# A gated linear attention and two-stage MoE kernel: half of each attention result computed on the other head's partitions and moved back by DMA

## The chip, the cores and the metric

The kernel runs on one core of a Trainium2 chip. A core has a matmul engine (TensorE, PE in the rows; its weight loads are PEld), three elementwise engines (VectorE = DVE, ScalarE = ACT, GpSimd = POOL), a queue engine that here issues nearly all transfers (SyncE = SP), and 16 DMA engines that move the data. The metric is device microseconds of one execution.

## The reference, cut to what matters

```python
for t in range(S):                                   # B=4, H=8, S=768, D=48
    state = alpha[:, :, t, :, None] * state + einsum('bhd,bhe->bhde', k[:, :, t], v[:, :, t])
    y[:, :, t] = einsum('bhd,bhde->bhe', q[:, :, t], state)
x = y.transpose(0, 2, 1, 3).reshape(3072, 384)
x = ((x @ w1) * (x @ w2)) @ w3 @ w_out               # widths 384 -> 1024 -> 1024 -> 384
p = probs / (probs.sum(-1) + 1e-9)
out = sum_e p[:, e] * (relu(x @ ew1[e]) @ ew2[e])    # 4 experts, 384 -> 1024 -> 384
```

## The kernel before

Every large product runs in three passes: a float32 operand is split into a high and a low part (hi by a copy on ACT, lo by a subtraction on DVE or POOL), and `mm3` (L86, L87, L88) adds hi*hi, lo*hi and hi*lo into one PSUM bank.

**Attention.** The sequence is cut into 24 chunks of 128 tokens (4 batches times 6). One chunk holds 8 heads as 4 pairs `p`; of a pair, head g=0 lies on partitions 0 to 63 and head g=1 on 64 to 127. A chunk is treated in two halves `t` of 64 tokens. For a chunk `i`: two scans on DVE give the decay products W (L574) and P (L582); k and q are scaled by them (`kW` L588, `qP` L592); k is transposed on PE (`kps`, L607) and copied (`kT`, L612); `u` (L632, tile `su`) makes the state updates and `scores` (L621, also `su`) makes q*k; DVE adds the updates into the states Zh and Z (L657, L664) and masks the scores into the tile `s` (L683). The output `y` (tile `yps`, one PSUM bank for each half t) gets two parts: `inter` (L673), old state times q, and `sv` (L691), masked scores times v. In `inter` head g reads its own partitions and writes its own partitions of `y`, and the loop has t outermost. ACT then copies y as the hi part (L707) and DVE subtracts for the lo part (L710), both straight into `xt`, the input of the next products. After a tile of three chunks, `pack` (L718) moves the padding rows of xt by six small DMAs, two for each of the three k-slices.

From chunk index 6 on (`GROUPED`) the PE work of a chunk comes as one group: `inter` of chunk i-1, `u` and `scores` of chunk i, `sv` of chunk i-1. There are 18 such chunks.

**First products.** A tile `j` of 384 tokens (8 tiles) gives 16 units of 9 matmuls (`abps`): x@w1 and x@w2 for 8 slices f. ACT copies a (L772), DVE multiplies (L776) into `g_sb`, which is stored to DRAM (`spilled`, L779). w1 and w2 arrive as wide words that are converted in 8 pieces on DVE and ACT (`c_m` L141, L142, L147; `w1h`, `w1l`, `w2h`, `w2l`), as later w_out and w3 (`wps`). Then `xps` makes x of the second stage, which is stored in sums as `kept`.

**Experts.** From about 440 us on the loop over 32 blocks (4 experts, 4 token tiles, 2 parts of the width) runs: `hps` are the first products by a scheme with fewer multiplications (the sums are on DVE, L1294), `ops` the second ones. The expert's weights are loaded, summed and split in `load_a`; the split goes in the pieces that `W_STEPS` lists (L1024, L1026). `checks` test that the inputs lie in the range that this fast path supports; `held_out` (L1160, L1161) reduces the outcome to one flag by a matmul into a bank of the `hps` pool, and at the very end all engines load that flag and branch.

**Order of the work.** Up to the expert loop a planner (`Plan`) sets each engine's instruction order: each operation has a cost and a due time made of the constants in the table at `TILE_DUE`; at each step it takes the ready operation with the earliest due time. The order is fixed when the program is built. The transfers of SP are one queue in that order, so an instruction that waits there holds all behind it.

## Time and profile before

| | |
|---|---|
| median of 3 runs | 1196.91 us (1194.83 to 1200.28) |
| the profiled execution's own time | 1197.35 us |
| its span, first to last instruction | 1195.5 us |
| PE busy | 1167.1 us, 98% |
| DVE, ACT, POOL busy | 69%, 52%, 37% |
| mean granted TensorE clock | 0.993 of full |

The span is what the profiler saw between the first and the last instruction; the execution's own time is 1.85 us longer. Busy shares are averages over stages, and a busy PE is a modelled figure (matmuls overlap), so stages and single chunks have to be read one by one.

### The profile page before, as it was taken

What the parts mean: (1) busy time and instruction counts of PE and PEld (TensorE: products, weight loads), DVE (VectorE), ACT (ScalarE), POOL (GpSimd) and SP (SyncE); (2) the same over time, 40 slices, a digit from 0 to 9 for tenths busy, and PEclk for the clock granted to TensorE, in tenths of its full rate; (3) what the DMA queues carried; (4) which work ended last, traced back from release to release, by engine and by line L of the source; (5) the groups of instructions that cost most, each with busy time, mean ns of one, the idle gap of its engine ahead of it and who ended that gap; (6) DMA issues with size and microseconds to landing.
All of it is one profiled execution on the core that took longest, in us unless ns stands there. A gap on an engine that the chain in (4) does not pass through costs nothing.

```text
span 1195.5 us, 24960 instructions
## 1 busy us (share of the span) xinstructions
PE 1167.1 (98%) x9186; PEld 1149.3 (96%) x9186; DVE 829.2 (69%) x1513; ACT 627.4 (52%) x1238; POOL 445.1 (37%) x517
## 2 busy tenths in 40 slices
PE   5899999999999999999999999999999999999997
PEld 4799999999999999999999999999999999999997
DVE  8898788966665856667677656667666587576563
ACT  4565555554544445454666655666565545444432
POOL 2133321010000006776744434744433655433332
PEclk9899999999999999999999999999999999999999
DMA  8756675555775696478576595695784863753821
GB/s 318 223 171 188 211 216 200 173 166 192 272 284 177 243 337 226 168 304 292 208 288 225 199 330 203 244 347 178 275 303 156 307 244 127 290 176 142 291 81 43
DMA packets 131171, 269.54 MB, mean 225 GB/s; under 512 B 17376, under 2 KB 64992, under 8 KB 131040
## 3 DMA queue, kind: packets, MB, share of 16 engines
q1 hardware_dynamic: 130176, 266.67, 63.8%
q8 instruction: 75, 1.23, 0.4%
q10 hardware_dynamic: 864, 1.18, 0.3%
q14 instruction: 56, 0.46, 0.1%
HBM read 207.24 MB, written 58.20 MB: 222 GB/s over the span
## 4 chain that ended last, share of the span: by engine, by line
PE 95%; DVE 3%; DMA 1%; issue 0%; POOL 0%; SPq 0%; ACT 0%; DVEq 0%; POOLq 0%
PE ops L87 11%; PE ops L86 11%; PE ops L88 11%; PE hps L86 9%; PE hps L87 9%; PE hps L88 9%; PE abps L86 6%; PE abps L87 6%; PE abps L88 6%; PE xps L86 3%; PE xps L88 3%; PE xps L87 3%; PE yps L673 2%; PE yps L691 1%; PE wps L86 1%; PE wps L88 1%
## 5 line engine op out<-in xcount | busy, mean ns | idle before, releaser
L1294 DVE TENSOR_TENSOR raw_x<-hps,raw_x 128x384 f32<-128x384 f32 x416 | 226.4, 554 | 212.3 <-PE hps L88 197.2
L1277 POOL TENSOR_TENSOR ht<-raw_x,ht 128x384 fp32r<-128x384 f32 x227 | 238.1, 1051 | 274.5 <-ACT raw_x L1276 222.2
L1275 ACT ACTIVATE ht<-raw_x 128x384 fp32r<-128x384 f32 x227 | 118.6, 523 | 228.3 <-DVE raw_x L1294 215.9
L87 PE MATMUL ops<-wb,ht 128*128 128x384 f32 x681 | 231.5, 340 | 0.0
L86 PE MATMUL ops<-wb,ht 128*128 128x384 f32 x681 | 230.8, 339 | 0.0
L88 PE MATMUL ops<-wb,ht 128*128 128x384 f32 x681 | 230.6, 339 | 0.0
L86 PE MATMUL hps<-xo,wa 128*128 128x384 f32 x640 | 217.8, 340 | 2.5 <-DVE raw_x L1294 1.2
L87 PE MATMUL hps<-xo,wa 128*128 128x384 f32 x640 | 215.5, 337 | 0.0
L88 PE MATMUL hps<-xo,wa 128*128 128x384 f32 x640 | 215.1, 336 | 0.0
L1294 DVE TENSOR_TENSOR raw_x<-raw_x,hps 128x384 f32<-128x384 f32 x256 | 136.5, 549 | 25.5 <-PE hps L88 25.1
L1276 ACT ACTIVATE raw_x<-raw_x 128x384 f32<-128x384 f32 x256 | 134.7, 526 | 8.1
L86 PEld LDWEIGHTS hps<-xo,wa 128*128 128x128 f32 x640 | 120.2, 188 | 8.4 <-DVE raw_x L1294 6.0
L86 PEld LDWEIGHTS ops<-wb,ht 128*128 128x128 f32 x681 | 128.0, 188 | 0.0
L88 PEld LDWEIGHTS ops<-wb,ht 128*128 128x128 f32 x681 | 127.9, 188 | 0.0
L87 PEld LDWEIGHTS ops<-wb,ht 128*128 128x128 f32 x681 | 127.5, 187 | 0.0
L87 PEld LDWEIGHTS hps<-xo,wa 128*128 128x128 f32 x640 | 120.2, 188 | 0.0
L88 PEld LDWEIGHTS hps<-xo,wa 128*128 128x128 f32 x640 | 120.1, 188 | 0.0
L1294 DVE TENSOR_TENSOR raw_x<-raw_x 128x384 f32<-128x384 f32 x128 | 88.6, 692 | 4.4
L698 POOL MEMSET Z<- 128x1 f32 x18 | 1.8, 98 | 191.7 <-PE yps L673 191.7
L1277 POOL TENSOR_TENSOR ho<-raw_x,ho 128x384 fp32r<-128x384 f32 x29 | 30.7, 1060 | 105.0 <-DMA xo<-kept 71.4
L86 PE MATMUL abps<-xt,w2h 128*128 128x384 f32 x192 | 66.0, 344 | 0.0
L86 PE MATMUL abps<-xt,w1h 128*128 128x384 f32 x192 | 65.9, 343 | 0.0
(136 smaller groups left out, 2224.2 us busy)
## 6 DMA issues: line engine op xcount, KB each, us to landing
xo<-kept SPq DMA_DIRECT2D x272, 384.0 KB, 6.4
kept<-ac SPq DMA_DIRECT2D x45, 384.0 KB, 2.9
partial<-ac SPq DMA_DIRECT2D x72, 192.0 KB, 1.9
ac<-partial SPq DMA_DIRECT2D x72, 192.0 KB, 6.4
spilled<-g_sb SPq DMA_DIRECT2D x64, 192.0 KB, 2.3
gg<-spilled SPq DMA_DIRECT2D x64, 192.0 KB, 3.3
c_raw<-in_w3T_dram SPq DMA_DIRECT2D x16, 512.0 KB, 4.1
raw_x<-in_w3T_dram SPq DMA_DIRECT2D x8, 1024.0 KB, 7.0
```

Source lines behind the costliest of these rows:

```text
L86: nc.tensor.matmul(out=ps, lhsT=lh, rhs=rh, start=first, stop=False)
L87: nc.tensor.matmul(out=ps, lhsT=ll, rhs=rh, start=False, stop=False)
L88: nc.tensor.matmul(out=ps, lhsT=lh, rhs=rl, start=False, stop=last)
L673: PE.matmul(out=r["y"][rows, p, t], lhsT=Z[rows, p], rhs=r["q"][rows, p, half], start=p == 0, stop=False)
L691: PE.matmul(out=r["y"][rows, p, t], lhsT=v[half, p, g], rhs=r["s"][half, g, p], start=first and t == 0 and p == 0, stop=p == NP - 1)
L698: G.memset(r["Zh"][:, NP - 1, 63:], 0.0)
L1275: A.activation(out=hh[:, 0], in_=s, func=ACTF.Relu)
L1276: A.activation(out=s, in_=s, func=ACTF.Relu)
L1277: G.tensor_tensor(out=hh[:, 1], in0=s, in1=f32(hh[:, 0]), op=ALU.subtract)
L1294: V.tensor_tensor(out=tmp[:, s], in0=ins[0], in1=ins[1], op=SIGN[op])
```

## The change

1. **Other head's partitions.** In grouped chunks, the second half's results (t=1) of head g are written on the partitions of the other head: `rows2[g ^ (t & grouped)]` in `inter` and `sv`. `inter` now goes over the heads outermost and the halves inside.
2. **Moving back.** The first half's hi and lo are made as before, 256 columns wide. The second half's go into the memory of the chunk's score tile `s`, which has been read by then (`turned`), and two DMAs on SP (`swap`) put them into xt. `masked` of the chunk after next, `pack` and the products wait for them.
3. **Weight splits** in 12 pieces instead of 8 (`W_STEPS`), with the loop's slots for them extended to 12.
4. **`held_out`** is called after the last matmul block instead of when the checks end.
5. **Last stores**: of the last six, three go on ACT's queue and three on SP's.
6. **A new table** of due times, which reorders all that the planner orders.

```diff
-W_STEPS = ((0, 0, 6), (0, 6, 12), (1, 0, 6), (0, 12, 16), (1, 6, 12), (0, 16, 20), (1, 12, 16), (1, 16, 20))
+W_STEPS = ((0, 0, 3), (0, 3, 6), (1, 0, 3), (0, 6, 9), (1, 3, 6), (0, 9, 12), (1, 6, 9), (0, 12, 16), (1, 9, 12),
+           (0, 16, 20), (1, 12, 16), (1, 16, 20))
...
-CHUNK_DUE = 72150.5
-ATT_DUE = -6421.33
+CHUNK_DUE = 81059.4
+ATT_DUE = 133025
...
-                n["u"] = n["scores"] = add("PE", (0.36 + 0.18 + 0.18 * (not last) + 0.47) + (1.39 if i > GROUPED else 0), due + U_DUE,
+                n["u"] = n["scores"] = add("PE", (0.36 + 0.18 + 0.18 * (not last) + 0.47) + (0.94 if i > GROUPED else 0), due + U_DUE,
...
-                for t, half in halves[first:]:
-                    Z = r["Zh"] if t else tiles[i - B]["Z"]
-                    for p, g, rows in heads:
-                        PE.matmul(out=r["y"][rows, p, t], lhsT=Z[rows, p], rhs=r["q"][rows, p, half],
+                for p, g, rows in heads:
+                    for t, half in halves[first:]:
+                        Z = r["Zh"] if t else tiles[i - B]["Z"]
+                        PE.matmul(out=r["y"][rows2[g ^ (t & grouped)], p, t], lhsT=Z[rows, p], rhs=r["q"][rows, p, half],
...
-            n["m"] = add("DVE", dve(512) + 0.07, due + M_DUE, masked, n["scores"], n.get("inter"), old(2, "sv"), port=False)
+            n["m"] = add("DVE", dve(512) + 0.07, due + M_DUE, masked, n["scores"], n.get("inter"), old(2, "sv", "swap"),
+                         port=False)
...
-                            PE.matmul(out=r["y"][rows, p, t], lhsT=v[half, p, g], rhs=r["s"][half, g, p],
+                            PE.matmul(out=r["y"][rows2[g ^ (t & grouped)], p, t], lhsT=v[half, p, g],
+                                      rhs=r["s"][half, g, p],
...
+            def parts():
+                x = tiles["x", j][:, :, :, o * C:(o + 1) * C].rearrange("p s n (t e) -> p s n t e", t=2)
+                if not grouped:
+                    return [(x, r["y"])]
+                turned = r["s"].rearrange("p g n e -> p (g n e)").bitcast(F32R).rearrange("p (s n e) -> p s n e", s=2, n=NP)
+                return [(x[:, :, :, 0], r["y"][:, :, 0]), (turned, r["y"][:, :, 1])]
...
-                A.activation(out=x[:, 0], in_=r["y"], func=ACTF.Copy)
+                for x, y in parts():
+                    A.activation(out=x[:, 0], in_=y, func=ACTF.Copy)
...
-                V.tensor_tensor(out=r["x"][:, 1], in0=r["y"], in1=f32(r["x"][:, 0]), op=ALU.subtract)
+                for x, y in parts():
+                    V.tensor_tensor(out=x[:, 1], in0=y, in1=f32(x[:, 0]), op=ALU.subtract)
+
+            def swap():
+                (x, _), (turned, _) = parts()
+                x = tiles["x", j][:, :, :, o * C + HC:(o + 1) * C]
+                for g in range(2):
+                    nc.sync.dma_start(out=f32(x[rows2[g]]), in_=f32(turned[rows2[1 - g]]))
...
+                if grouped:
+                    n["swap"] = add("SP", 2 * 0.65, due + HI_DUE, swap, n["lo"], kib=256)
...
-            x_in = [at[i][k] for i in range(j * CPT, (j + 1) * CPT) for k in ("pack", "lo") if k in at[i]]
+            x_in = [at[i][k] for i in range(j * CPT, (j + 1) * CPT) for k in ("pack", "lo", "swap") if k in at[i]]
...
             V.tensor_reduce(out=over, in_=excess, axis=mybir.AxisListType.X, op=ALU.add)
-            yield
-            held_out()
...
-                (nc.scalar if t == NT2 - 1 else nc.sync).dma_start(out=out[r * 128:(r + 1) * 128], in_=ac)
+                (nc.scalar if t == NT2 - 1 and m % 2 == 0 else nc.sync).dma_start(out=out[r * 128:(r + 1) * 128], in_=ac)
...
             second(*block)
+        held_out()
```

Of the new table only two lines are shown; its effect is seen in the orders. On PE, where the third tile (j=2, chunks 6 to 8) begins, the order of before has 63 `abps` matmuls between the groups of chunks 10 and 11; `Z_106` and `Z_110` are the two states that `inter` of chunk 10 reads (below, its end; further `abps` rows are left out):

```order
L691 MATMUL yps<-s,rv 64x64 x16
L86 MATMUL abps<-xt,w1h 128x384
...
L607 MATMUL kps<-ident,rk 128x128 x4
L673 MATMUL yps<-rq,Z_106 64x64 x8
L673 MATMUL yps<-rq,Z_110 64x64 x8
L632 MATMUL su<-rv,kT 64x48 x16
L621 MATMUL su<-rq,rk 64x64 x16
L691 MATMUL yps<-s,rv 64x64 x16
```

The order of the change has the same place, with the two groups back to back and two transposes between them:

```order
L633 MATMUL su<-rv,kT 64x48 x16
L622 MATMUL su<-rq,rk 64x64 x16
L693 MATMUL yps<-s,rv 64x64 x16
L608 MATMUL kps<-ident,rk 128x128 x8
L674 MATMUL yps<-rq,Z_106 64x64
L674 MATMUL yps<-rq,Z_110 64x64
...
L633 MATMUL su<-rv,kT 64x48 x16
L622 MATMUL su<-rq,rk 64x64 x16
L693 MATMUL yps<-s,rv 64x64 x16
L87 MATMUL abps<-xt,w1h 128x384
```

The group of chunk 11 has moved ahead of the third tile's first products (ten units, 90 matmuls, now follow it), and `inter` alternates between the two states, which is the alternation between the halves.

On SP's queue at the same place, before (the names in brackets are the semaphores that the issue waits for):

```order
L553 DMA rk<-in_kT_dram 128x512 [waits DMAHW0_49]
L718 DMA xt<-xt 16x2x384 [waits DMAHW1_49,DVE_49]
L718 DMA xt<-xt 16x2x384 [waits DMAHW2_49]
L718 DMA xt<-xt 16x2x384 [waits DMAHW3_49]
L718 DMA xt<-xt 16x2x384 [waits DMAHW4_49]
L718 DMA xt<-xt 16x2x384 [waits DMAHW5_49]
L718 DMA xt<-xt 16x2x384 [waits DMAHW6_49]
```

and with the change:

```order
L727 DMA xt<-s 64x8x64 [waits DMAHW5_49,DVE_49,Activation_49]
L727 DMA xt<-s 64x8x64 [waits DMAHW6_49]
L799 DMA spilled<-g_sb 128x384 [waits DMAHW7_49,DVE_49]
L1134 DMA p_sb<-in_probs_dram 128x24x4 [waits DMAHW0_49]
L735 DMA xt<-xt 16x2x384 [waits DMAHW5_49,DMAHW1_49]
L735 DMA xt<-xt 16x2x384 [waits DMAHW6_49,DMAHW2_49]
L735 DMA xt<-xt 16x2x384 [waits DMAHW3_49]
L735 DMA xt<-xt 16x2x384 [waits DMAHW4_49]
L735 DMA xt<-xt 16x2x384 x2
L799 DMA spilled<-g_sb 128x384 [waits DMAHW7_49,DVE_49]
L727 DMA xt<-s 64x8x64 [waits DVE_49,DMAHW0_49,PE_49,Activation_49]
L727 DMA xt<-s 64x8x64 [waits DMAHW1_49]
```

The six DMAs of `pack` waited for DVE's lo part; now they wait for the landing of the two swaps ahead of them, and the swaps wait for DVE.

On DVE, ahead of the first products of the kernel (the end of chunk 3's lo part, `xt`, and what stands beside it), before:

```order
L683 TENSOR_TENSOR s<-su,mask 128x512
L141 TENSOR_SCALAR c_m<-c_raw 128x768
L142 SCALAR_TENSOR_TENSOR c_m<-c_raw,c_m 128x768
L657 TENSOR_TENSOR Z_110<-su,Z_105 128x4x48
L664 TENSOR_TENSOR Z_109<-su,Z_110 128x4x48
L710 TENSOR_TENSOR xt<-yps,xt 128x4x128
L582 SCALAR_TENSOR_TENSOR P<-ra,edge 128x520
```

and with the change:

```order
L684 TENSOR_TENSOR s<-su,mask 128x512
L583 SCALAR_TENSOR_TENSOR P<-ra,edge 128x520
L658 TENSOR_TENSOR Z_110<-su,Z_105 128x4x48
L665 TENSOR_TENSOR Z_109<-su,Z_110 128x4x48
L721 TENSOR_TENSOR xt<-yps,xt 128x4x128
L96 TENSOR_TENSOR w1l<-c_m,w1h 128x3x256
```

Chunk 5's scan P has moved ahead of chunk 3's lo part, and the low part of the first weights (`w1l`), which stood well ahead of it, now follows it; the second conversion (`c_m`) is further up.

## Rows read from the trace of the kernel before

**Rows 1.** The page, part 1: busy us, share of the span, instructions.
```profile
PE 1167.1 (98%) x9186; PEld 1149.3 (96%) x9186; DVE 829.2 (69%) x1513; ACT 627.4 (52%) x1238; POOL 445.1 (37%) x517
```

**Rows 2.** Windows: stretch, its length, busy PE, PEld, DVE, ACT, POOL, clock, DMA.
```profile
100.00:200.00 100.00, 100.00 (x1604) 96.99 (x1603) 81.56 (x142) 55.46 (x130) 27.16 (x36) 1.00 0.69 209
...
600.00:800.00 200.00, 200.00 (x1133) 198.33 (x1132) 135.97 (x253) 118.62 (x214) 97.59 (x115) 1.00 0.71 257
```

**Rows 3.** Waits of PE: us in total, times, longest.
```profile
PE yps L673 <- DVE xt L710: 6.8, 4, 2.8
...
PE hps L86 <- DVE held L1161: 0.5, 1, 0.5
```

**Rows 4.** The chain that ended last, one attention group: start, us, what.
```profile
84.06 1.01 PE yps L673 x29
...
85.53 0.48 PE su L621 x28
86.07 0.47 PE yps L691 x30
86.54 0.38 PE abps L86
...
91.42 0.44 PE kps L607 x4
...
103.26 0.47 PE yps L691 x30
...
111.54 0.38 PE abps L86
```

**Rows 5.** Groups by line and form: busy us, mean ns, idle before.
```profile
L710 DVE TENSOR_TENSOR xt<-yps,xt 128x512 fp32r<-128x512 f32 x24 | 16.4, 684 | 4.8 <-ACT xt L707 4.5
L707 ACT ACTIVATE xt<-yps 128x512 fp32r<-128x512 f32 x24 | 14.3, 596 | 23.9 <-PE yps L691 22.0 <-PE abps L87 0.9 <-DMA ra<-in_aT_dram 0.9
...
L657 DVE TENSOR_TENSOR Z<-su,Z 128x192 f32<-128x192 f32 x20 | 7.0, 351 | 9.9 <-PE su L621 9.9
...
L655 ACT ACTIVATE Z<-su 128x192 f32<-128x192 f32 x4 | 1.3, 319 | 1.2 <-PE su L621 1.1
```

**Rows 6.** Timeline of PE: two starts, nine matmuls apart.
```profile
53.47 0.33 PE L86 MATMUL abps<-xt,w1h 128*128 128x384 f32 x1
...
55.03 0.34 PE L86 MATMUL abps<-xt,w2h 128*128 128x384 f32 x1
```

**Rows 7.** SP's timeline at the third tile; landing times of pack; issues.
```profile
105.40 4.16 SPq L718 DMA_DIRECT2D xt<-xt  x6
...
DMA to landing us min/median/max: 2.1/2.5/4.9
...
rv<-in_vP_dram SPq DMA_DIRECT2D x24, 256.0 KB, 3.9
...
p_sb<-in_probs_dram SPq DMA_DIRECT2D x1, 48.0 KB, 4.0
```

**Rows 8.** Timeline of DVE and of PE before the first products.
```profile
25.77 1.31 DVE L95 TENSOR_TENSOR w1l<-c_m,w1h 128x768 fp32r<-128x768 f32 x1
...
38.11 0.68 DVE L710 TENSOR_TENSOR xt<-yps,xt 128x512 fp32r<-128x512 f32 x1
38.71 1.23 DVE L582 TENSOR_TENSOR_SCAN P<-ra,edge 128x520 f32<-128x520 f32 x1
...
38.94 1.97 PE L673 MATMUL yps<-rq,Z 64*64 64x64 f32 x32 [0.52 <-DVE xt L710]
40.84 0.69 PE L86 MATMUL abps<-xt,w1h 128*128 128x384 f32 x1
```

**Rows 9.** Groups by line and form: the split of an expert's weights on DVE.
```profile
L1024 DVE TENSOR_TENSOR wa<-araw,wa 128x768 fp32r<-128x768 f32 x10 | 9.4, 951 | 0.0
```

**Rows 10.** Timeline of the end, DVE and ACT's queue.
```profile
1189.00 0.61 DVE L1246 SCALAR_TENSOR_TENSOR ac<-ops,p_sb,ac 128x384 f32<-128x384 f32 x1
1189.02 1.91 ACTq L1250 DMA_DIRECT2D out_dram<-ac  x4
```

More of the change, by code (lines that the diff above doesn't have):

```diff
@@ L334 @@
 MM = 0.174
[L335 to L381 removed]
+TILE_DUE = 145492
+CHUNK_DUE = 81059.4
+ATT_DUE = 133025
+START_DUE = -9.24766e+07
+START_STEP = 2.61366e+06
+NEXT_DUE = -8.97403e+06
+NEXT_STEP = 12775.5
+LOAD_DUE = 146577
+UNIT_DUE = 24975.8
+ZS_DUE = -994399
+CHECK_DUE = 890180
+KT_DUE = -87820.2
+U_DUE = -43145.3
+Z_DUE = -968641
+M_DUE = -11914.3
+KW_DUE = -4.37131e+06
+QP_DUE = 1.74468e+06
+HI_DUE = 5223.09
+SC_DUE = 178459
+IN_DUE = -335253
+CONV_DUE = 106678
+CONV_STEP = 9690.71
+RAW_DUE = -7.01133e+06
+WO_DUE = 1.2661e+08
+W3_DUE = 742416
+W3_STEP = 939.36
+WL_DUE = 674141
+WL_STEP = 1.47992e+07
+XS_DUE = -26816.4
+XS_STEP = 193058
+XT_DUE = 204116
+XT_STEP = 674192
+XU_DUE = 834547
+XU_STEP = 79170.5
+X0_DUE = 207605
+X1_DUE = 283836
+X2_DUE = -94266.6
+X3_DUE = -5397.31
+X4_DUE = 1.18092e+06
+X5_DUE = 10660.2
+X6_DUE = 912612
+X7_DUE = 852795
+XA_DUE = 207213
+XL_DUE = 1.26613e+08
+XL_STEP = 2.34819e+07
+G_LEAD = 1.27588e+06
+FIRST_DUE = 28655.7
 EARLY = 3
@@ L721, in rest @@
             def rest():
-                n["hi"] = add("ACT", act(512), due + HI_DUE, hi, n["sv"], ab_done.get(j - 2))
-                n["lo"] = add("DVE", dve(512), due + HI_DUE, lo, n["hi"], port=False)
+                n["hi"] = add("ACT", (1 + grouped) * act(512 // (1 + grouped)), due + HI_DUE, hi, n["sv"], ab_done.get(j - 2))
+                n["lo"] = add("DVE", (1 + grouped) * dve(512 // (1 + grouped)), due + HI_DUE, lo, n["hi"], port=False)
+                if grouped:
+                    n["swap"] = add("SP", 2 * 0.65, due + HI_DUE, swap, n["lo"], kib=256)
                 if o == CPT - 1:
-                    n["pack"] = add("SP", 6 * 0.65, due + HI_DUE, pack, [at[k]["lo"] for k in range(i - CPT + 1, i + 1)],
+                    n["pack"] = add("SP", 6 * 0.65, due + HI_DUE, pack,
+                                    [at[k].get("swap", at[k]["lo"]) for k in range(i - CPT + 1, i + 1)],
                                     kib=288)
@@ L735, in final @@
                     sv()
-                n["inter"] = n["sv"] = add("PE", 2.1, due + HI_DUE, final, n["m"], n["Zh"], n["qP"], old(1, "lo"))
+                n["inter"] = n["sv"] = add("PE", 1.65, due + HI_DUE, final, n["m"], n["Zh"], n["qP"], old(1, "lo"))
                 rest()
@@ L1213, in gated_attention_moe_kernel @@
                     job(load_a(e, k), (i0 - 4 + k, 18), *((i0 - 3 + k, g) for g in range(19)),
-                        *((i0 - 1 + k, g) for g in (1, 2, 3, 4, 5, 6, 7, 9)))
+                        *((i0 - 1 + k, g) for g in range(1, 13)))
                 job(load_b(e, 0), (i0 - 1, 0))
```

46 lines of the change are left out of this document (removed).

## The prediction

> **What bounds the kernel now.** I read the page's first part, then the windows, then PE's waits, then the chain. The first part says that PE is busy for 1167.1 us, 98% of the span, and that no other engine comes near it [rows 1]. The windows say where: from 100 to 200 us, where attention runs between the first products, and from 600 to 800 us, in the expert loop, PE has no idle time at all, while DVE has 18 us and 64 us of it in the same stretches [rows 2]. What is left for others is the start. The longest waits of `inter` on DVE's lo part sum to 6.8 us in 4 waits [rows 3], and the one of them that I show ends at 38.9 us [rows 8]. So the rule for this kernel is simple: in the first 40 us DVE counts, at the very end the last stores count, and in between a microsecond taken off PE's instructions is a microsecond of the kernel, as long as the new order doesn't make PE wait.
>
> **Part 1, `inter` on four quadrants.** One group, in the chain: `inter` 1.01 us, `scores` 0.48, `sv` 0.47, and with `u` from 84.06 to 86.54, that is 2.48 us [rows 4]. `inter` and `sv` are alike in number and shape (16 matmuls of 64x64, two passes each), yet `inter` takes twice as long. What differs is where they lie: `inter` alternates between two quadrants of the array (head 0 to its own partitions, head 1 to its own), and both neighbours write the same bank; `scores` and `sv` go round all four quadrants. The change sends `inter` round all four and alternates the banks. `sv` keeps four. I take the 0.48 of `scores`, whose loop (pair, head, half) is the nearest to the new one: 0.53 us less for a chunk, 18 chunks, **-9.5 us**. Bounds: 0.47 as `sv` would give -9.7; if the quadrants aren't the reason, 0.
>
> The Trainium skill, "TensorEngine Tiling (Array Packing)", has two sentences for this. Under "Key Properties" different tiles run in parallel, and by that alone the two diagonal quadrants of before should have overlapped already, which 1.01 against 0.47 [rows 4] denies. Under "Restrictions and Gotchas" different row tiles can't access one PSUM bank at the same time, and this fits the trace: before, neighbours of different row tiles share a bank. After it each bank is still written from both row tiles, two matmuls apart, so by that rule only neighbours overlap: half of 1.01 is 0.505, a sum of 9.1 us in place of 9.5.
>
> **Part 2, hi and lo in two halves.** DVE takes 351 ns for 192 columns and 684 for 512 [rows 5], about 418 for 256, so twice 418 in place of 684: 0.15 us more. ACT takes 319 and 596 [rows 5], about 374 for 256: also 0.15 more. Over 18 chunks that is 2.7 us on each engine, in a stage where DVE has 18 idle us in a hundred and ACT 44 [rows 2]: nothing on the path, except inside the chain of part 3.
>
> **Part 3, swap and pack at a tile's start.** Before, the way from a tile's last `sv` to its first product was: `sv` ends at 103.26 + 0.47 = 103.7, hi and lo, six pack issues on SP from 105.40 for 4.16 us, and PE reaches the tile at 111.54 without a wait [rows 4, 7]. With the change the swaps stand between lo and pack. For the third tile, from the end of its last `sv` (T): hi and lo in halves, behind a masked multiply, end at about T+2.5; two swap issues, for which I take 0.65 us each, a sixth of the pack's 4.16 being 0.69; landing. No row has 128 KB from partition to partition in 256-byte runs. Bounds: 2.5 us, the median of pack's 48 KB [rows 7], and 4.9, its maximum; the loads of 256 KB take 3.9, and the 48 KB of `p_sb` in 16-byte runs, six times as many pieces, take 4.0 [rows 7]. I take 3.5, between pack and loads, nearer to the loads since it moves half of what they move. So swap lands at T + 2.5 + 0.65 + 3.5 = T+6.6. Pack's last issue begins five steps of 0.69 later and lands 2.5 after: T+12.6. PE needs that last k-slice after six of the unit's nine matmuls; nine take 55.03 - 53.47 = 1.56 us [rows 6], so six take 1.04, and PE may start the tile at T+11.6.
>
> What PE has to do until then, by the order of the change: a transpose, 27 products (4.7), the group of chunk 10 (2.48 - 0.53 = 1.95), two transposes and the group of chunk 11. With 0.44 us for a transpose [rows 4] that is 0.44 + 4.7 + 1.95 + 0.88 + 1.95 = 9.9 us. Also the second transpose must wait for ACT's copy of the first, which stands behind chunk 9's hi: about 0.75 + 0.6 by [rows 5], 1.2 us of idle PE after the overlap. That makes 11.1, against 11.6: 0.5 more. **+1.7 us** here. Bounds: 0.8 (the copy alone, 0.6 and its hand-overs) and 5.1 (swap and pack both at 4.9: T+16.4 minus 1.04 minus 9.9, rounded). The other tiles have more to do in between: by the same count over the order, 12.2 us at the fourth tile (54 products, a group, two transposes), 13.8 at the fifth, 18 at the sixth, 12.0 at the eighth, against 11.6. They don't wait at 3.5, but their spare time is 0.4 to 2.2 us in three of them. For these, for the masked multiply that now waits for the swap of two chunks before, and for stores and loads held on SP behind waiting packs I add **+0.5**; bounds 0 and 3.
>
> **Part 4, weight splits.** A piece of 768 columns takes DVE 0.951 us [rows 9]; by the slope between the two widths in [rows 5] a cut in two adds 0.15. There are 8 weight halves with two cuts on each engine, 2.4 us on DVE in 740 us. PE waits for nothing from 600 to 800 us and DVE has 64 idle us there [rows 2], which is the cover. Nothing.
>
> **Part 5, the flag.** Its matmul takes a bank that the next `hps` waits for: 0.5 us of PE [rows 3], gone: **-0.5**. At the end it costs no PE time on the path: PE's last matmul is over before DVE's last 0.61 us starts at 1189.00 [rows 10], and the flag's small DVE instruction comes behind that, beside the last store.
>
> **Part 6, last stores.** DVE is done at 1189.61, but ACT's queue issues its last four stores from 1189.02 to 1190.93, 0.48 each [rows 10]. On an empty SP queue the last issue can begin at about 1189.7 and end at 1190.2: **-0.7**. Bounds -0.9 and +0.5 (if loading the flag, now last, outlasts the store).
>
> **Part 7, the start.** The first products begin at 40.84, behind `inter` of chunk 4 (1.97 us), which waits for chunk 3's lo part, 38.11 on DVE [rows 8]. Up to that lo part DVE has, by the orders, the same work as before but one more scan P (1.23) and one less `w1l` (1.31) [rows 8]: -0.1. `w1l` now follows, 0.95 to 1.31 us, under the 1.97 us of `inter`. So 0; bounds -2 (idle gaps filled) and +2 (scans slowed beside POOL, weights late).
>
> **Sum.** -9.5 + 1.7 + 0.5 - 0.5 - 0.7 = -8.5 us on the profiled execution's own 1197.35: 1188.85 us, say 1188.8. That execution is 0.4 us above the median of 1196.91, so the step from the median is 8.1 us, 0.7%. A measurement of this kernel can tell about 0.5% from no change, 6 us, that is a time under 1190.9.
>
> **Rivals.**
> A. *Waits eat a third to a half of the gain.* Swaps land at 4 to 5 us, two or three tile starts wait 1 to 2 us each, and the group of chunk 11 waits longer. For it: small spare times (above). Against it: PE works ahead of most tiles. 3 us more than forecast, to 6: 1191 to 1195.
> B. *The start gains too.* DVE's idle gaps at the start close and the weights come earlier: 2 to 4 us more, 1185 to 1187. Against it: the first products still stand behind the same chain on DVE.
> C. *`inter` stays at 1.01.* Each bank is still written from both row tiles; if any such sharing serializes, or four quadrants aren't what makes `scores` short, the 9.5 us go: 1188.8 + 9.5 = 1198.3. Against it: `sv` and `scores` at half the time [rows 4]. The tiling page's bank rule, read strictly, is the nearest to this.
> D. *Slower: the swap chain decides every tile.* SP can't pass a waiting pack, so a slow swap delays all that follows. If pack and swap both land at 4.9 and an issue of 64 partitions in 8 runs takes 1.6 us, a tile may start at about T+18: 6 us late at the third, 5.8 at the fourth, 4.2 at the fifth, 6 at the eighth, 22 together, 1188.8 - 2.2 + 22 = 1208.6. It passes the time of before when the chain is some 3 us longer than mine. For it: the runs are 256 bytes, and the row of 4.9 exists [rows 7]. Against it: `p_sb` with far smaller runs lands in 4.0 [rows 7].
> The Trainium skill, "DMA: Bandwidth & Descriptors", section "Specifications", says that transfers below 512 B per piece lose line rate to a read-modify-write. No row here times such a run between partitions; it would lengthen the landing in A and D.
>
> **Chances.** Forecast 0.62 (1186 to 1191), A 0.20, B 0.08, C 0.05, D 0.05. Faster by over 0.5%: nearly all of the forecast and B, 0.70. Within 0.5%: most of A, all of C and the edge of the forecast, 0.25. Slower by over 0.5%: 0.05, D. The range 1184.5 to 1194.5 leaves out C, D, and the ends of A and B.
>
> **What would show it.** `inter` in the chain at 0.5 and not 1.0; an idle PE of 1 to 3 us before the group of chunk 11 or the third tile, with ACT's `kT`, DVE's lo part or a DMA as releaser, and nothing like it at the other tiles; swap landings near 3.5; no wait on `held` near 960 us; the first products at 39 to 43 us. The prediction is wrong if `inter` stays above 0.7, if idle PE between 60 and 440 us sums to more than 5 us, or if the first products come more than 3 us off.

## The result and the profile after

The change makes the kernel slower: 1210.4 us (median of 6 runs, 1207.13 to 1212.3) against 1197.68 us (6 runs) for the kernel before, a ratio of 1.0103, 95% interval 1.0083 to 1.0123. The forecast was 1188.8, in a range of 1184.5 to 1194.5. The profiled execution after took 1207.13 us, its span 1205.1 us at a mean clock of 0.995.

The page's first part, after [rows 1]:

```profile
PE 1162.1 (96%) x9186; PEld 1143.4 (95%) x9186; DVE 838.8 (70%) x1547; ACT 629.8 (52%) x1272; POOL 444.7 (37%) x517
```

PE has 5.0 us less to do, and the span is 9.6 us longer: PE waits. Where it waits is seen in the two windows that had none before [rows 2]: 5.8 us in the attention, 4.1 us in 200 us of the expert loop.

```profile
100.00:200.00 100.00, 94.17 (x1339) 89.96 (x1339) 76.49 (x143) 49.86 (x121) 18.30 (x27) 0.98 0.82 221
600.00:800.00 200.00, 195.87 (x1110) 194.47 (x1110) 135.52 (x253) 118.10 (x216) 96.61 (x114) 1.00 0.70 255
```

**What the products gained.** The chain through an attention group, after [rows 4]: start, us, what.

```profile
82.58 0.62 PE yps L674 x32
83.21 0.45 PE su L633 x32
83.66 0.48 PE su L622 x32
84.14 0.47 PE yps L693 x32
```

From 82.58 to the end at 84.61 it is 2.03 us, where it was 2.48: 0.45 less, over 18 chunks 8.1 us.

**What the attention lost.** PE's timeline from 95 to 200 us, only the rows with more than 0.3 us of idle time before them (in brackets: idle us and what ended it):

```profile
108.08 0.63 PE L608 MATMUL kps<-ident,rk 128*128 128x128 f32 x4 [0.78 <-ACT kT L613]
111.78 0.33 PE L693 MATMUL yps<-s,rv 64*64 64x64 f32 x5 [0.94 <-issue]
140.79 0.69 PE L693 MATMUL yps<-s,rv 64*64 64x64 f32 x31 [2.44 <-POOL rv L702]
141.92 0.36 PE L693 MATMUL yps<-s,rv 64*64 64x64 f32 x1 [0.44 <-issue]
...
176.15 0.69 PE L693 MATMUL yps<-s,rv 64*64 64x64 f32 x32 [0.59 <-POOL rv L702]
```

The longest, 2.44 us, ends with a memset of POOL that takes 0.1 us itself. It stands in POOL's queue behind the scaling of the next k and q, and those wait for their loads; POOL's timeline there:

```profile
138.09 1.18 POOL L589 TENSOR_TENSOR rk<-rk,W 128x512 f32<-128x512 f32 x1 [7.75 <-DMA rk<-in_kT_dram]
139.50 1.17 POOL L593 TENSOR_TENSOR rq<-rq,P 128x512 f32<-128x512 f32 x1 [0.22 <-DMA rq<-in_qT_dram]
...
140.64 0.10 POOL L702 MEMSET rv<- 128x1 f32 x1
```

The idle time has an echo, in the windows right behind it (length, busy PE, clock, DMA share, GB/s):

```profile
138.00:140.00 2.00, 0.35 (x25) 1.00 1.18 250
140.00:145.00 5.00, 3.77 (x41) 0.69 0.24 55
```

After 2.4 idle us PE's granted clock falls to 0.69 of full in the mean of these 5 us, that is most of them at 1.2 GHz in place of 2.4; nine products of that stretch take 0.32 us each or more, where they take 0.17 at full clock. This echo is not in every profile: e2 has none between 60 and 440 us, e3 and e12 have twice as much of it, so it moves the end of this stage by 0 to 3.4 us from profile to profile. The moves themselves, in the view of the tile that they read (`s`), on SP:

```profile
L727 SPq DMA_DIRECT2D xt<-s x36: 602/628/1915, 88.5 to 359.3; - x36
...
  DVE s L684: 6.7, 4
...
DMA to landing us min/median/max: 2.7/4.5/7.7
```

They land 4.5 us after issue in the middle, 1.0 above the 3.5 that was taken, and up to 7.7; DVE's masking waits 6.7 us for them.

**What the loop lost.** PE's waits over the span (us, times, longest):

```profile
PE hps L87 <- DVE raw_x L1312: 9.9, 10, 1.8
```

The wait on `held` [rows 3] is gone as forecast, but the hidden products now wait for DVE's sums `raw_x`, 8.7 us of it in 9 waits between 600 and 1020 us, where before had none. One of the nine, in the chain that ended last, and the same place in DVE's timeline:

```profile
631.01 0.79 DVE raw_x L1312
631.80 1.42 DVE wa L1044
633.22 0.48 DVE raw_x L1312
633.74 0.44 PE hps L87
```

```profile
629.83 0.68 DVE L1044 TENSOR_TENSOR wa<-raw_x,wa 128x512 fp32r<-128x512 f32 x1
630.43 0.55 DVE L1312 TENSOR_TENSOR raw_x<-hps,raw_x 128x384 f32<-128x384 f32 x1
631.01 0.79 DVE L1312 TENSOR_TENSOR raw_x<-raw_x 128x384 f32<-128x384 f32 x1
631.73 1.50 DVE L1044 TENSOR_TENSOR wa<-raw_x,wa 128x512 fp32r<-128x512 f32 x1
```

The last two weight pieces (`wa`, 512 columns) now stand among the block's sums. Each takes DVE 0.7 to 1.5 us at a place where PE needs the sum behind it to get a bank back.

**The tail.** From the end of the last `ac` step to the end of the span it is 5.9 us before (1189.61 to 1195.5) and 9.5 after:

```profile
1192.37 3.27 DVE L1264 SCALAR_TENSOR_TENSOR ac<-ops,p_sb,ac 128x384 f32<-128x384 f32 x6 [10.57 <-PE ops L89]
1195.55 0.14 DVE L1181 TENSOR_SCALAR held<-fps 1x1 int32<-1x1 f32 x1
```

So three places, with one theory for each: the *place* of the last weight pieces, the *late flag*, and the *moves*. The rivals were the number of pieces, the two store queues, and the new order of the work.

### The profile page after: what moved, and what is told of

The parts are those of the page before. It is cut to its first block, busy times and chain, and to the rows that moved or that the text cites. A ratio compares the mean times of both kernels' runs of the same rounds, so it can differ in the third digit from the quotient of the medians.

```text
span 1205.1 us, 25115 instructions
## 1 busy us (share of the span) xinstructions
PE 1162.1 (96%) x9186; PEld 1143.4 (95%) x9186; DVE 838.8 (70%) x1547; ACT 629.8 (52%) x1272; POOL 444.7 (37%) x517
## 4 chain that ended last, share of the span: by engine, by line
PE 89%; DVE 6%; DMA 2%; issue 1%; ACT 1%; POOL 0%; DVEq 0%; SPq 0%; POOLq 0%
PE ops L88 11%; PE ops L87 11%; PE ops L89 11%; PE hps L87 9%; PE hps L88 9%; PE hps L89 9%; PE abps L87 5%; PE abps L88 5%; PE abps L89 5%; PE xps L87 3%; PE xps L88 3%; PE xps L89 3%; DVE raw_x L1312 2%; PE yps L693 1%; PE yps L674 1%; PE wps L87 1%
## 5 line engine op out<-in xcount | busy, mean ns | idle before, releaser
L593 POOL TENSOR_TENSOR rq<-rq,P 128x512 f32<-128x512 f32 x24 | 35.7, 1488 | 91.4 <-DVE P L583 35.3
L1310 ACT ACTIVATE raw_x<-hps 128x384 f32<-128x384 f32 x96 | 46.7, 488 | 38.5 <-PE hps L89 35.8
```

Source lines behind the costliest of these rows:

```text
L593: G.tensor_tensor(out=r["q"], in0=r["q"], in1=r["P"][:, :, 1:C + 1], op=ALU.mult)
L1310: A.activation(out=tmp[:, s], in_=ps, func=ACTF.Copy)
```

## The experiments

Three numbers of each profile are used: the first hidden product (the end of attention and first products), the loop from there to the end of the last `ac` step, and the tail. Before: 440.1, 749.5 and 5.9 us. Changed: 438.4, 757.2 and 9.5. A profile is one execution, and the first of the three numbers moves by some us between executions of one order of work (437.0 to 442.2 us in seven profiles, below); the medians of all runs are given beside it.

### The weight splits

**e1**, the splits of before in the changed kernel:

```diff
-W_STEPS = ((0, 0, 3), (0, 3, 6), (1, 0, 3), ...            # 12 pieces
+W_STEPS = ((0, 0, 6), (0, 6, 12), (1, 0, 6), ...           # 8 pieces
-                        *((i0 - 1 + k, g) for g in range(1, 13)))
+                        *((i0 - 1 + k, g) for g in (1, 2, 3, 4, 5, 6, 7, 9)))
```

> The changed kernel with the weight splits of before: eight pieces, none later than the ninth group of a block. If the late splits cause the expert loop's loss, the waits of the hidden products on DVE raw_x fall from 9.9 us to about 1.2 and the time from the first hidden product to the last ac step from 756.6 to about 748.5: about 1202 us in all (8 below the changed kernel). If the loss in the loop comes from DMA traffic or from another order of the work ahead of it, the loop stays at 755 to 757 us and the time at 1209 to 1211.

Measured: 1196.98 us, ratio to before 1.0004 (0.9989 to 1.0019). The loop takes 749.1 us and PE waits for nothing in it from 470 us on. The same place of DVE's timeline holds sums alone:

```profile
630.01 0.55 DVE L1311 TENSOR_TENSOR raw_x<-hps,raw_x 128x384 f32<-128x384 f32 x1
630.60 1.12 DVE L1311 TENSOR_TENSOR raw_x<-raw_x 128x384 f32<-128x384 f32 x1
631.64 1.24 DVE L1311 TENSOR_TENSOR raw_x<-hps,raw_x 128x384 f32<-128x384 f32 x2
```

The loop's 8 us are the splits'. The time fell by more than that, since the tail also came down, to 6.5 us (below).

**e3**, the small pieces in the groups of before, in an order in which two small ones stand where before had one large one:

```diff
-W_STEPS = ((0, 0, 3), (0, 3, 6), (1, 0, 3), (0, 6, 9), (1, 3, 6), (0, 9, 12), (1, 6, 9), (0, 12, 16), (1, 9, 12),
+W_STEPS = ((0, 0, 3), (0, 3, 6), (0, 6, 9), (0, 9, 12), (1, 0, 3), (1, 3, 6), (0, 12, 16), (1, 6, 9), (1, 9, 12),
            (0, 16, 20), (1, 12, 16), (1, 16, 20))
...
-                        *((i0 - 1 + k, g) for g in range(1, 13)))
+                        *((i0 - 1 + k, g) for g in (1, 1, 2, 2, 3, 3, 4, 5, 5, 6, 7, 9)))
```

> The changed kernel with its twelve small pieces, but issued in the groups in which before issued its eight (two small pieces in a row where before had one large one), so that the last falls in the ninth group again. If the place in the block costs the time, as I hold, the loop takes 748 to 750 us and the kernel about 1202 to 1203. If the number of pieces costs it (12 fixed costs where there were 8), the loop stays above 754 us and the kernel at about 1208 to 1210.

Measured: 1200.6 us, ratio 1.0032 (1.0018 to 1.0046). The loop takes 753.0 us, between the two expectations; of the 8.7 us of waits for `raw_x` 2.6 are left, 3 of 9. Each of the three comes behind two small pieces in a row on DVE (0.55 and 1.38 us, from 619.67 us on for the first). Place is most of it, and two pieces in a row make a new bad place.

**e6**, the change's splits alone on the kernel before (the edit of e1 reversed):

> The kernel before with only the change's weight splits: twelve pieces in the groups 1 to 12 of a block. If these splits by themselves cost the expert loop its 8 us, with none of the new attention, PE waits for raw_x about 9 times for 8 to 10 us between 600 and 1100, and the time is 1204 to 1206 us (ratio 1.006 to 1.008). If they do so only together with the other edits, it stays within 1 us of before.

Measured: 1206.67 us, ratio 1.0091 (1.0074 to 1.0108). PE's waits:

```profile
PE hps L87 <- DVE raw_x L1295: 11.5, 10, 2.9
```

**e7**, before with its eight large pieces, the last two moved:

```diff
-                        *((i0 - 1 + k, g) for g in (1, 2, 3, 4, 5, 6, 7, 9)))
+                        *((i0 - 1 + k, g) for g in (1, 2, 3, 4, 5, 6, 11, 12)))
```

> The kernel before with its eight large pieces, the last two issued in the groups 11 and 12 instead of 7 and 9. If the place of the last pieces decides, the waits for raw_x come as with the small ones in two of three blocks or more: 5 to 8 us, 1201 to 1205 us. If the number of pieces decides, PE does not wait and the time stays within 1 us of before.

Measured: 1204.37 us, ratio 1.0070 (1.0055 to 1.0086). PE's waits from 470 us on:

```profile
PE hps L86 <- DVE raw_x L1294: 7.1, 6, 1.6
```

Number and size of the pieces are those of before, so the place alone costs 7.3 us of the 9.6.

### The flag, the stores, the tail

**e2**, the flag back where the checks end, in the changed kernel; **e5**, the flag late, in the kernel before (the reverse):

```diff
             V.tensor_reduce(out=over, in_=excess, axis=mybir.AxisListType.X, op=ALU.add)
+            yield
+            held_out()
...
-        held_out()
         in_range = nc.values_load(held, min_val=0, max_val=1)
```

> The changed kernel with the flag's product and compare back where the checks end, the last stores still on two queues. If the late flag makes the tail longer, the span from the last ac step to the end falls from 10.1 us to about 6.3, and a wait on held of 0.5 us comes back at 960: about 1207 us (3 to 3.5 below the changed kernel). If the two queues of the last stores, or their landing, cause the tail, it stays at about 10 and the time at 1210 to 1211.

> The kernel before with one edit: the flag's product and compare moved behind the last stores. In two profiles of the changed kernel's family the tail (end of the last ac step to the end of the span) was 6.6 us with the late flag, where before has 5.9, and in one 9.5. If the late flag costs what the first of these say, the wait on held of 0.5 us goes, the tail is 6.5 to 6.7, and the time is the same within 0.5 us. If the late flag is what makes the tail 9.5, the time is 3 us above before (1199 to 1200).

Measured: e2 1209.26 us, ratio 1.0113 (1.0098 to 1.0128), tail 7.9 us. e5 1196.74 us, ratio 0.9999 (0.9990 to 1.0008), tail 6.6 us. In the kernel before, the late flag makes the tail 0.7 us longer and takes the wait of 0.5 us away: it costs nothing that can be measured, and my theory of 3 us falls. In the changed kernel the early flag takes 1.6 us off the tail of the one profile, and the medians don't show it.

**e12**, the changed kernel once more:

> The changed kernel once more. If its long tail (9.5 us from the end of the last ac step to the end of the span, where three kernels with the same late flag have 6.6) is its own, it comes again at 9 to 10 us and the span is 1205 to 1208 us; if it was chance in one run, the tail is 6.6 us and the span about 1202 us.

Measured: 1208.7 us, ratio 1.0098 (1.0080 to 1.0115), tail 9.7 us. The long tail is the kernel's own.

**e17**, the last stores on one queue, and **e18**, twelve more small instructions on DVE and on ScalarE ahead of everything:

```diff
-                (nc.scalar if t == NT2 - 1 and m % 2 == 0 else nc.sync).dma_start(out=out[r * 128:(r + 1) * 128], in_=ac)
+                (nc.scalar if t == NT2 - 1 else nc.sync).dma_start(out=out[r * 128:(r + 1) * 128], in_=ac)
```

```diff
-        V.memset(mid, -(RANGE[0] + RANGE[1]) / 2)
+        for _ in range(13):
+            V.memset(mid, -(RANGE[0] + RANGE[1]) / 2)
...
-        A.activation(out=over, in_=one, func=ACTF.Copy)
+        for _ in range(13):
+            A.activation(out=over, in_=one, func=ACTF.Copy)
```

> The changed kernel with its last six stores on ScalarE's queue alone, as before. If the two queues end the kernel earlier, as predicted (0.7 us), this is 0.5 to 1 us slower than the changed kernel (tail 10 to 10.5 us, about 1210 us). If the long tail comes from the code that is fetched at the end (59 fetches in the three profiles with tails of 7.9 to 9.7 us, 56 to 58 in all with 5.8 to 6.7 us), then a program that is a few instructions shorter on SyncE may fall back to 58 fetches and a tail of 6.6 us: about 1207 us.

> The changed kernel with twelve more small instructions each on DVE and ScalarE at its start (one of theirs repeated), nothing else. If the long tail depends on where the last code lies in what is fetched, the tail changes by 1 us or more (6.6 or 10.5 to 11 us instead of 9.6); if it comes from the work of the kernel, it stays at 9.4 to 9.8 us.

Measured: e17 1212.68 us, ratio 1.0126 (1.0109 to 1.0143), tail 9.7 us; e18 1209.39 us in its one run, tail 9.5 us. The queues don't make the tail. The interval of e17 overlaps those of the changed kernel, so a gain of two queues isn't shown.

What makes the tail long has one place, in the trace's full list of SP's instructions (the views leave out those that only wait). At the end SP goes through a row of waits for its queues. In the changed kernel it stands still for 2.8 us between two of them, from 4.8 to 7.6 us after the last `ac` step, though the last store had landed at 2.0; in e3 the same step takes under 0.1 us. The six profiles with a tail of 7.9 us and more (changed, e2, e12, e15, e17, e18) have such a pause, of 1.7 to 3.2 us, and the 14 with 5.8 to 6.7 us have none. In all six it stands ahead of the same number, SP's 1649th instruction, although their lists of SP's instructions have three lengths (1661, 1663, 1668). The 14 others end before that number (1601 to 1646 instructions), or reach it right behind the branch on the flag, where every engine pauses for 3 us or more in any case (1669), or shortly before it (e3, 1673, without a pause).

So the 3 us hang on where SP's program ends: the moves make it 67 instructions longer than before's 1601, and e1, one instruction longer still, is past the place. e18 lengthened the programs of DVE and ScalarE, not SP's, and changed nothing. That SP waits there for its next code fits this, but is not shown. The count of code packets on queue 14 in the page's third part (59 or 60 in the six, 56 to 58 in the 14), which I took for the sign, proves nothing by itself: it counts up to the end of the span, and in e3 and e14 one more packet comes 2.1 and 1.6 us behind that end.

### The moves

In these, all but e4 have the splits of before too, so that e1 is what they stand against (first hidden product 439.2 us, 1197.0 us).

**e4** and **e13**, the second half's results left where they lie, without the 36 transfers; e4 with the change's splits, e13 with those of before:

```diff
-                turned = r["s"].rearrange("p g n e -> p (g n e)").bitcast(F32R).rearrange("p (s n e) -> p s n e", s=2, n=NP)
-                return [(x[:, :, :, 0], r["y"][:, :, 0]), (turned, r["y"][:, :, 1])]
+                return [(x[:, :, :, t], r["y"][:, :, t]) for t in range(2)]
...
-                for g in range(2):
-                    nc.sync.dma_start(out=f32(x[rows2[g]]), in_=f32(turned[rows2[1 - g]]))
+                pass
```

> The changed kernel without the moving: the second half-chunk's results are rounded and stored where they lie, and the 36 transfers that move them to the other head's partitions are left out (so the result is another one), with the same order of all other work. If these transfers and what queues behind them cost the attention its gain, PE's idle time from 100 to 200 us falls from 5.8 us to about 1 and the first hidden product comes at 432 to 434 us instead of 438.4: about 1204 us. If the new order of the work causes the idle time by itself, the first hidden product stays at 437 to 439 us and the time at 1209 to 1211.

> The changed kernel with the weight splits of before and with the results left where they lie, no transfers at all (the output is another one): what the attention and the splits could give if the moving cost nothing. By the 5 to 6 us that leaving the transfers out gave with the small splits: first hidden product at 432 to 434 us, about 1191 us. If that gain came from something in that one run, 438 us and 1197 us.

Measured: e4 1200.06 us, ratio 1.0032 (1.0019 to 1.0046), first hidden product at 432.9 us; e13 1192.98 us, ratio 0.9968 (0.9955 to 0.9982), at 434.1 us. The order is the same in both as with the moves. PE in e4 (windows, as above):

```profile
100.00:200.00 100.00, 97.98 (x1386) 95.12 (x1379) 84.06 (x153) 54.54 (x132) 23.20 (x31) 1.00 0.69 208
```

Of the 5.8 us of idle PE 3.8 go with the transfers, and the clock stays at 1.00. The other 2.0 us (2.9 in e13) are there without them: 0.78 us for the copy of `kT` at 108 us, 0.8 (1.3) us in the middle of an `sv` near 112 us, which the profile puts down to nothing (`issue`), and smaller ones.

**e8**, the moves on ScalarE's queue:

```diff
-                    nc.sync.dma_start(out=f32(x[rows2[g]]), in_=f32(turned[rows2[1 - g]]))
+                    nc.scalar.dma_start(out=f32(x[rows2[g]]), in_=f32(turned[rows2[1 - g]]))
```

> The changed kernel with the weight splits of before (its first hidden product came at 439.2 us) and with the 36 moving transfers issued from ScalarE's queue instead of SyncE's, at the same place in the order. If the moves cost by holding up the loads and stores behind them in SyncE's queue (1.3 us of issue each pair, and the wait for the rounding), most of the 5.5 us that leaving them out gave comes back: first hidden product at 434 to 436 us, about 1192 to 1194 us. If they cost by their own landing (4.5 us in the middle) and by sharing the DMA engines, it stays at 438 to 440 us and the time within 1.5 us of the kernel without this edit (1197).

Measured: 1201.39 us, ratio 1.0041 (1.0026 to 1.0055), 4.4 us above e1; PE idles 7.9 us from 100 to 200, and the first hidden product comes at 447.6 us, past both expectations. DVE's masking waits 9.6 us for the moves, where it waited 4.5 in e1. What holds them up on ScalarE's queue was not taken apart; SP's queue was the better one.

**e9**, the results on their way in memory of the w3 weights instead of in `s`, so that the masking waits for no transfer (the last chunks' results overwrite finished parts of these weights, so the output is another one; the work is the same):

```diff
-                turned = r["s"].rearrange("p g n e -> p (g n e)").bitcast(F32R).rearrange("p (s n e) -> p s n e", s=2, n=NP)
+                turned = wts[2, i % 2].rearrange("p f d -> p (f d)")[:, 2048 + i // 2 % 2 * 512:][:, :512].rearrange(
+                    "p (s n e) -> p s n e", s=2, n=NP)
```

> The changed kernel with the weight splits of before, and the results on their way are kept in four places of the idle w3 weights instead of in the buffer of the masked scores, so that the masking two chunks later waits for no transfer; same order, same transfers. If that wait (4.8 us on DVE at 100 to 125 us, and what it makes late) is how the moves cost, PE's idle time from 100 to 200 us falls from 6.0 us to 1.5 to 3, the first hidden product comes at 434 to 436 us, and the time is 1192 to 1194 us. If the transfers cost by their traffic or their issues, it stays at 438 to 440 us and at 1196 to 1198 us.

Measured: 1196.3 us, ratio 0.9995 (0.9985 to 1.0006), first hidden product at 438.6. DVE's wait for the moves is gone (3.8 us in e1 at that place), PE's idle time is not, 5.8 us:

```profile
100.00:200.00 100.00, 94.24 (x1334) 90.10 (x1333) 76.13 (x142) 49.48 (x120) 18.58 (x27) 0.97 0.79 216
```

The wait I had taken for the cause isn't it.

**e10**, **e14**, **e15**: the results lie where they are, and transfers run that nobody needs, of the same pieces (e10), in pieces of 2 KB (e14), or of one eighth of the size (e15):

```diff
+                away = wts[2, i % 2].rearrange("p f d -> p (f d)")[:, 2048 + i // 2 % 2 * 512:][:, :512]
...
+                    nc.sync.dma_start(out=f32(away[rows2[g]]), in_=f32(x[rows2[1 - g]]))             # e10
+                    nc.sync.dma_start(out=f32(away[rows2[g]]), in_=s[rows2[1 - g]])                  # e14
+                    nc.sync.dma_start(out=f32(away[rows2[g], 0, 0]), in_=f32(x[rows2[1 - g], 0, 0])) # e15
```

> As with the results left where they lie (first hidden product at 432.9 us), with the weight splits of before, but all 36 transfers are issued, of the same size and pieces, from the results to four places of the idle w3 weights: nobody waits for their landing but the queue (the output is another one). If landing and waits cost the time, this comes out as without the transfers: 432 to 434 us, about 1191 to 1192 us in all. If their traffic and their 1.3 us of issue per pair cost it, it comes out as with them: 438 to 440 us, about 1197 us.

> As e13, but with 36 transfers of 128 KB that nobody needs, as in the run of moves to nowhere, now in pieces of 2 KB instead of 256 bytes (64 packets each instead of 512; the output is another one). If the number of small pieces is the cost, this comes out near no transfers: first hidden product at 432 to 435 us, 1191 to 1193 us. If bytes or issues cost it, as the moves to nowhere did: 438 to 441 us, 1197 to 1199 us.

> As e13, but with 36 transfers that nobody needs of one eighth of the size (64 pieces of 256 bytes, 16 KB each; the output is another one). If the issues on SyncE's queue and its waits for the rounding cost the time, it stays at 438 to 441 us and 1197 to 1199 us; if pieces or bytes cost it, it comes out near no transfers, 432 to 435 us and 1191 to 1193 us.

Measured: e10 1198.91 us, ratio 1.0016 (1.0005 to 1.0028); e14 1199.58 us, 1.0024 (1.0010 to 1.0038); e15 1196.09 us, 0.9998 (0.9989 to 1.0007). First hidden products at 441.3, 440.1 and 434.2 us. Windows of e14, then of e15:

```profile
100.00:200.00 100.00, 93.47 (x1339) 90.33 (x1338) 76.41 (x143) 50.36 (x123) 18.64 (x27) 0.97 0.76 220
```

```profile
100.00:200.00 100.00, 95.73 (x1364) 92.49 (x1363) 81.62 (x147) 51.92 (x126) 20.98 (x29) 1.00 0.70 208
```

In e10, somebody does wait, against what was expected: the transfers read the padding rows that `pack` (L734) overwrites, and SP holds `pack` for their landing. SP's waits in e10:

```profile
SPq L734 <- DMA w3l<-xt: 10.1, 3, 5.3
...
SPq L734 <- DMA w3h<-xt: 5.1, 3, 3.2
```

So e10 doesn't tell waiting from traffic, but e14 against e15 does. In e14, which reads `s`, `pack` waits for none of the transfers, the masking for 0.7 us and others for under 2; it costs as much as the moves all the same. In e15 `pack` waits 8.1 us for them, as in the changed kernel (7.5), and most of the cost is gone. Their size costs: from e15 to e14 5.9 us at the first hidden product (2.4 of it idle time of PE, the rest mostly the low clock behind it) and 3.5 in the medians, 5.0 without the 1.5 us by which e15's tail is longer (8.1 us, the pause above). The issues with their waits cost less: e15 stands 3.1 us above e13 in the medians, these 1.5 included. 64 pieces of 2 KB cost as much as 512 of 256 bytes.

**e16**, a complete kernel with the results laid out by half-chunk, so that a move has 64 pieces of 2 KB:

```diff
-        xt2 = xtp.tile([128, 2, 2, NP, TT], F32R, tag="xt", name="xt")
+        xt2 = xtp.tile([128, 2, TT // HC, 2, NP, HC], F32R, tag="xt", name="xt")
...
-                x = tiles["x", j][:, :, :, o * C + HC:(o + 1) * C]
+                x = tiles["x", j][:, 2 * o + 1]
```

> The changed kernel with the weight splits of before, complete, with the attention's results laid out by half-chunk (high and low part and all heads of a half in a row of 2 KB), so that the moves go in 64 pieces of 2 KB instead of 512 of 256 bytes; the packing goes in more pieces (192 of 256 bytes per transfer instead of 32 of 1.5 KB), the first products read the results in six runs of 64. If the small pieces cost the attention its gain, the moves land in 2 to 3 us instead of 4.6 and the first hidden product comes at 433 to 436 us: 1191 to 1194 us, faster than both kernels. If issues or bytes cost it, 438 to 440 us and about 1197 us.

Measured: 1198.34 us, ratio 1.0011 (1.0000 to 1.0021); the moves land in 4.4 us (4.7 in e1), and PE idles 6.8 us from 100 to 200. No gain, in agreement with e14. The Trainium skill, "DMA: Bandwidth & Descriptors", section "Why small descriptors are slow (HBM only)", says that transfers from SBUF to SBUF don't suffer from small pieces; e16 against e1 bears it out, and e10 against e14 too, though these two also differ in who waits.

**e11**, `inter` half by half instead of head by head:

```diff
-                for p, g, rows in heads:
-                    for t, half in halves[first:]:
+                for p in range(NP):
+                    for t, half in halves[first:]:
...
+                        for g, rows in enumerate(rows2):
```

> The changed kernel with the weight splits of before and the products of inter issued half by half (both heads of a half, then the other half) where the change has head by head; the results are the same ones. Neighbours then lie on diagonal quadrants, and two in a row write one bank. If four quadrants work at once whatever the order, inter stays at 0.62 us; if neighbours share time only on quadrants of one row or one column, as the 1.01 us of before suggests, it goes to 0.8 to 1.0; if the bank that both row halves write in turn is what keeps it from the 0.47 us of the others, it falls to about 0.5.

Measured: 1199.06 us in its one run, and `inter` in the chain is 0.62 us, as in the change:

```profile
85.23 0.62 PE yps L674 x32
```

Neighbours on one diagonal and one bank, as in before, but with the other diagonal next: no loss. This alone doesn't clear the banks, since the pairs still alternate between two of them. The chunks ahead of the grouped ones do: in the changed kernel their `inter` goes head by head too and alternates the banks, but stays on the two old quadrants. Chunk 5 in before, then in the changed kernel, then a grouped chunk's `inter` and `sv` there (start, us from the first start to the last end):

```profile
46.77 1.15 PE L673 MATMUL yps<-rq,Z 64*64 64x64 f32 x32 [1.56 <-DVE xt L710]
```

```profile
43.73 1.17 PE L674 MATMUL yps<-rq,Z 64*64 64x64 f32 x32 [1.56 <-DVE xt L721]
...
82.51 0.69 PE L674 MATMUL yps<-rq,Z 64*64 64x64 f32 x32
...
83.96 0.65 PE L693 MATMUL yps<-s,rv 64*64 64x64 f32 x32
```

Alternating banks on two quadrants gains nothing. What cost 1.01 us was having only two quadrants, not the order of the banks.

## Why the prediction was wrong

**Part 1, `inter`: right in kind, 1.4 us too large.** 0.45 us a chunk instead of 0.53, 8.1 in place of 9.5. The 0.15 us by which `inter` stays above `sv` lie at its start, not in its steps: by the start times in the trace, the 32 passes of either begin in fours 58 ns apart (in twos in before's `inter`), but the first four of `inter`, behind a wide product, take about 0.1 us. The Trainium skill's rule in "TensorEngine Tiling (Array Packing)", section "Restrictions and Gotchas", that different row tiles can't access one bank at the same time, would have given 9.1 by the prediction's reading. The trace doesn't bear it out as the price here: alternating banks gained nothing in chunk 5, and `inter`, whose banks are each written from two row tiles, steps as fast as `sv`, whose banks are each written from one.

**Part 2, halves: right.** The two forms of lo take 416 and 415 ns; 418 was the estimate.

**Part 3, moves: failed, by its bounds.** I priced the chain of one tile's start (+1.7, at most 5.1) and gave the rest 0.5. At the third tile PE idles 0.78 us for `kT` and 0.94 in an `sv`, 1.72 in all, and that this is the forecast is luck: 1.2 was taken for the copy and 0.5 for `pack`, the 0.94 has no releaser in the profile, and `pack` cost nothing. It landed 1.1 us later than the sum had it, at 113.01 us, and PE needed its last slice at 113.26. What failed is the 0.5 for everything else, with its bound of 3: the new attention makes PE idle 5.3 to 7.0 us between 100 and 200 us in seven profiles (changed, e1, e2, e3, e12, e17, e18), and the low clock behind the idle time costs 1.7 us more in the changed kernel (3.4 us at half speed). The sign that was to mean wrong came true, too: idle PE between 60 and 440 us sums to 6.8 us, over 5.

I looked for the price in who waits for the moves. The experiments put it elsewhere: 4.7 MB more to carry (36 times 128 KB) share the DMA engines with the loads and stores of a stage in which PE runs without slack. The stores of `g_sb` land in 2.6 to 3.0 us in the seven profiles, in 2.3 to 2.5 with the old attention (before, e5, e6, e7), and in 2.1 and 2.5 without the moves (e4, e13). The loads of k don't tell them apart in the middle (4.2 to 4.5 against 4.0 to 4.5). At the stall at 140 us the load of v landed 4.0 to 6.4 us after the end of its issue in the seven profiles, 6.6 in e14, 2.8 in e4, 4.4 in e13 and 5.1 in e15. That a load that lands later makes the stall follows from POOL's rows above; how the bytes make transfers late was not taken apart further.

Together: first hidden products at 440.1, 437.8, 437.5 and 438.7 us with the old attention (before, e5, e6, e7), and at 438.4, 438.1, 439.2, 437.0, 438.8, 442.2 and 440.6 with the new (changed, e12, e1, e2, e3, e17, e18). The attention's gain is eaten whole, which is more than rival A had it eat. Rival D had the sign and the sort of cause, but not the place: it wanted the moves late at every tile's start. That its 1208.6 us lies near the measured 1210.4 is luck, since most of the loss is that of the splits. Two sums of this part are off by their own terms, without effect on the forecast: the bound of 5.1 comes to 5.5, and rival D's 6 us at the third tile to 6.9.

**Part 4, weight splits: failed, the largest term.** "Nothing", with DVE's 64 idle us of 200 as cover. Idle time in the mean is no cover at a place: in groups 11 and 12 of a block DVE works sums off that PE is waiting for, and pieces of 0.7 to 1.5 us there made PE wait 0.3 to 1.8 us, nine times. The step that failed is taking idle time in the mean for cover: the term was put at 0 and cost 9.6 us alone (e6), 7.3 of them for the place alone (e7). I counted the cuts and didn't look where the longer list of groups put them.

**Part 5, flag: right in the loop, small at the end.** The wait is gone, the tail is 0.7 us longer (e5). **Part 6, stores:** -0.7 isn't shown (e17). The tail's other 3 us had no term; they are SP's pause at a fixed place of its program.

**Part 7, start: right.** `inter` of chunk 4 took 1.97 us in before's profile [rows 8] because the clock was low there (0.50); in e5, e6 and e7, with the same order, it takes 1.15 us, and first products come at 38.7 to 39.7 us, about as after (38.77).

The sum as measured: the splits 9.6, the attention about 0, flag and wait about 0, the rest of the tail 3: 12.6 us, for 12.7 between the medians.

No complete kernel came out measurably faster than before. e13, which leaves the moves out, shows what is left: with free moves the new attention would give 3.6 us (0.3%), not 8.

## What to carry to other kernels

- Ask of extra work on a half idle engine at which place in the loop it lands and who waits for the instruction behind it, not how much idle time the window has; moving two large pieces cost 7 us, cutting them smaller 2 more.
- Where an engine runs without slack, price a transfer by its bytes against the stage's other transfers too, not only by who waits for it. Take the transfer out, then put it back with nobody waiting and, once more, with few bytes: this tells waiting from traffic, if the trace confirms that nobody waits.
- A longer program can cost at a place that has nothing to do with its work: ask in the trace where the last engine stood still before you blame the last edit.
- One profile can have a slow start by chance: compare two positions in the trace over several kernels that share the code up to there.

## What the runs showed of the hardware

- Between partitions, 128 KB in 512 pieces of 256 bytes land after 4.5 us in the middle (2.7 to 7.7), in 64 pieces of 2 KB after 4.4 (e16).
- Products of 64x64 on two diagonal quadrants: 1.01 us for 16, and no less with alternating banks (chunk 5: 1.17 us from first start to last end against 1.15); round all four: 0.62, in either order (e11).
- After 2.4 us without work PE's clock was granted at 0.69 in the mean over the next 5 us. Not after every such pause: in e6 PE idled 2.9 us at 798.8 us, and the clock stayed at 1.00.
- The time from the last computing step to the end of the span is 5.8 to 6.7 us in 14 profiles and 7.9 to 9.7 us in 6. The 6 have a pause of SP of 1.7 to 3.2 us ahead of its 1649th instruction, whatever their length. Why it pauses there is open.
